# Two attention chunks in one row-tiled group, and PSUM banks named one by one, in a fused retention + MLP kernel

## The chip, the cores and the metric

The kernel runs on one core of a Trainium2 chip. The metric is the time of one execution on the device in microseconds (us). Smaller is better.

## The reference, cut to what matters

```python
# q, k, v: [B=8, H=8, S=576, D=64];  w_in: [512, 2048];  w_out: [2048, 512]
scores = (q @ k.T) / 8                            # per batch and head
ret    = scores * where(i >= j, gamma_h ** (i - j), 0)
x      = (ret @ v), heads side by side            # [4608 tokens, 512]
out    = gelu_exact(x @ w_in) @ w_out             # [4608, 512]
```

The kernel computes the retention part in chunks of 128 positions. A sequence of 576 has four full chunks and a short one of 64, so there are 40 chunks in all. Within a chunk it forms scores and multiplies them by v (the *inner* part). What came before the chunk enters through a running sum of k^T v (the *cross* part). The MLP goes through the 4608 tokens in nine blocks of 512, numbered 0 to 8.

## The kernel before

Three terms are needed. *PSUM* is where TensorE's results lie; the pools below share out its eight banks (2 + 2 + 1 + 3). *Row-tiled* means that a matmul uses 64 of the array's 128 rows, so that two of them, here of an even and an odd head, run side by side. The *mode* of the array is the rows*columns in use, as the profile prints it: 128*128 for the MLP and the inner parts, 64*128 for scores and cross parts, and 64*64 for those of short chunks.

TensorE's instructions come out in an order that a small scheduler in the kernel chooses while the program is built. It lays attention steps between MLP steps. Its kinds are T (turn q and k), R (scores), S (inner part and running sum), U (a cross part alone), V (scale v), X (turn x, for the first chunks) and the MLP steps "1" and "2". Cuts are marked with `...`.

```python
ps_sc  = tile_pool("ps_sc",  bufs=2, space=PSUM)   # two banks: scores of even and odd heads
ps_out = tile_pool("ps_out", bufs=1, space=PSUM)   # two banks: inner + cross of one chunk
ps_u   = tile_pool("ps_u",   bufs=1, space=PSUM)   # one bank: running sum
ps_mlp = tile_pool("ps_mlp", bufs=3, space=PSUM)   # three banks, oldest first: hT and oT

def scores(i):                                     # 64 rows of the array: row-tiled
    sc = [ps_sc.tile([128, HP, 128], FP32, tag="sc", ...) for e in range(2)]
    for hp in range(HP):
        for e in range(2):
            sl = slice(64 * e, 64 * e + 64)
            nc.tensor.matmul(sc[e][:cs, hp, :cs], lhsT=qkT[sl, 1, hp, :cs], rhs=qkT[sl, 0, hp, :cs], ...)

def cross(i):                                      # 64 rows as well
    for hp in range(HP):
        for e in range(2):
            sl = slice(64 * e, 64 * e + 64)
            nc.tensor.matmul(ov[:cs, e, hp, :], lhsT=s["qkT"][sl, 0, hp, :cs],
                             rhs=s["u"][sl, hp, 64 * e:64 * e + 64], start=False, ...)

def mlp1_step(t, m, lo, hi):                       # 16 tiles hT a block, 4 matmuls each
    hT = ps_mlp.tile([128, TOK_BLK], FP32, tag="mlp", name="hT")
    ...
    nc.scalar.activation(g_tiles[t, m][:, lo:hi], hT[:, :hi - lo], AF.Gelu)

def mlp2_step(t, ts, m0, m1):                      # 4 pieces of 128 tokens, 16 matmuls each
    if m0 == 0:
        acc[t, ts] = ps_mlp.tile([128, d_model], FP32, tag="mlp", name="oT")
    ...
    if m1 == N_DF:
        nc.scalar.copy(o_sb, oT)
        nc.sync.dma_start(out[row0:row0 + 128, :], o_sb)

# in the scheduler: one chunk's scores, then the cross part of the chunk before it
elif kind == "R":
    sc = scores(i)
    ...
    if open_ is not None:
        cross(open_)
    masked(i, sc)                                  # VectorE: scores to SBUF, masked
    ...
    if open_ is not None:
        close(open_)                               # VectorE: o_ps to SBUF, then transposed by DMA
```

## Time and profile before

| | |
|---|---|
| time | 315.15 us, median of 3 runs (314.97 to 315.23) |
| span of the profiled execution | 313.4 us |
| TensorE (PE) busy | 304.2 us, 97% |
| share of the chain that ended last on PE | 94% |

First come lines of the page of the kernel before: busy time and share of each engine, then the busy tenths of 40 slices, then the chain that ended last. PEld is TensorE's loading of weights, DVE is VectorE, ACT is ScalarE and POOL is GpSimd.

```profile
span 313.4 us, 6167 instructions
...
PE 304.2 (97%) x2522; PEld 166.3 (53%) x2522; DVE 102.9 (33%) x189; ACT 141.2 (45%) x279; POOL 112.3 (36%) x144
...
PE   7889998999999999999999999999999999999996
...
DMA  9999999999999999999989999698321221020012
...
PE 94%; DVE 3%; DMA 1%; issue 1%; ACT 0%; SPq 0%; DVEq 0%
```

A busy PE is not yet a PE at its peak, so the starts have to be read as well. Next is the timeline of the kernel before, PE alone, around the group of one full chunk. The columns are start (us from the span's start), duration (us), engine, line, operation, output and inputs, rows*columns of the array in use, shape and count. Here sc are scores, o_ps is a chunk's output, hT belongs to the first product of the MLP and oT to the second.

```profile
144.56 0.38 PE L323 MATMUL oT<-w_out_203,g_2374 128*128 128x512 bf16 x1
144.78 0.38 PE L323 MATMUL oT<-w_out_203,g_2381 128*128 128x512 bf16 x1
145.09 0.23 PE L211 MATMUL sc_2426<-qkT 64*128 64x128 bf16 x1
145.10 0.23 PE L211 MATMUL sc_2427<-qkT 64*128 64x128 bf16 x1
145.16 0.22 PE L211 MATMUL sc_2426<-qkT 64*128 64x128 bf16 x1
...
145.33 0.28 PE L262 MATMUL o_ps<-u_sb,qkT 64*128 64x64 bf16 x8
145.54 0.39 PE L323 MATMUL oT<-w_out_179,g_2211 128*128 128x512 bf16 x1
145.77 0.38 PE L323 MATMUL oT<-w_out_179,g_2218 128*128 128x512 bf16 x1
```

Read the starts, not the durations. Two 512-column matmuls start 216 ns apart (144.56 to 144.78). From the last of them to the first scores it is 312 ns, about 96 ns more. Scores start in twos, one for each half of the rows (145.09 and 145.10). At the group's end eight small matmuls take 213 ns, though a pair of them inside the group takes some 28 ns. That is the price of a change of the array's mode, paid on the way in and again on the way out. The Trainium skill, "TensorEngine Tiling (Array Packing)", Key Properties, says that changing the tiling mode drains TensorE; this trace fits that, with a loss of about 0.1 us at each change.

Last, the chain of waits of the kernel before at the passage from the first to the second product of block 7 (start, duration, engine, tile, line, count). PE follows PE with no other engine in between.

```profile
265.12 0.24 PE o_ps L262 x8
265.37 3.56 PE hT L296 x16
268.93 13.81 PE oT L323 x64
282.74 13.81 PE hT L296 x64
```

### The profile page before, as it was taken

The page shows a single profiled execution, that of the slowest core. Times are in us where ns is not written, and L with a number is a line of the kernel's source. Part 1 is how long each engine was busy: PE and PEld are TensorE (multiplying, and loading weights), DVE is VectorE, ACT ScalarE, POOL GpSimd, SP SyncE. Part 2 cuts the span into 40 slices and gives each one's busy share as a digit, 9 for nine tenths or more (in the row PEclk, how much of TensorE's full clock was granted, in tenths as well). Part 3 has the DMA queues.
Part 4 walks back from the last instruction along what each step waited for, and adds up shares of the span by engine and source line. Part 5 has one row for each costly group of instructions (what it writes and reads, how often), then busy time and mean ns, then how long its engine had stood idle before and what let it go on. Part 6 is the DMA issues. An engine that isn't in the chain of part 4 may idle for free.

```text
span 313.4 us, 6167 instructions
## 1 busy us (share of the span) xinstructions
PE 304.2 (97%) x2522; PEld 166.3 (53%) x2522; DVE 102.9 (33%) x189; ACT 141.2 (45%) x279; POOL 112.3 (36%) x144
## 2 busy tenths in 40 slices
PE   7889998999999999999999999999999999999996
PEld 3568655985645444444454444444454444444444
DVE  3740256737644334433142334423242322000000
ACT  5668303773427621662256224632564245316611
POOL 9956879384384074093309230440000000000000
PEclk9999999999999999999999999999999999999999
DMA  9999999999999999999989999698321221020012
GB/s 139 149 190 194 182 164 199 171 148 132 216 152 156 154 152 183 164 157 149 195 131 130 122 165 135 87 145 155 84 44 29 82 76 19 24 85 37 0 60 74
DMA packets 168636, 39.40 MB, mean 126 GB/s; under 512 B 157600, under 2 KB 164128, under 8 KB 168608
## 3 DMA queue, kind: packets, MB, share of 16 engines
q0 software_dynamic: 115792, 17.97, 87.4%
q1 hardware_dynamic: 52816, 21.05, 37.2%
q8 instruction: 19, 0.31, 0.4%
q14 instruction: 9, 0.07, 0.1%
HBM read 36.70 MB, written 9.44 MB: 147 GB/s over the span
## 4 chain that ended last, share of the span: by engine, by line
PE 94%; DVE 3%; DMA 1%; issue 1%; ACT 0%; SPq 0%; DVEq 0%
PE hT L296 40%; PE oT L323 39%; PE o_ps L242 3%; PE u_ps L248 2%; PE o_ps L262 2%; DMA k_101<-in_k_dram 1%; PE qk_ps L198 1%; PE oT L313 1%; DVE vh L227 1%; PE x_ps L284 0%; PE warm L434 0%; DVE ret_974 L220 0%; DVE ret_895 L220 0%; DVE ret_431 L220 0%; DVE ret_297 L220 0%
## 5 line engine op out<-in xcount | busy, mean ns | idle before, releaser
L135 POOL DMA_DIRECT2D qk_ld<-in_q_dram x39 | 33.8, 866 | 84.7 <-DMA qkT<-qk_ld 60.5
L327 ACT COPY o_sb<-oT 128x512 f32<-128x512 f32 x35 | 20.3, 587 | 93.6 <-PE oT L323 93.6
L135 POOL DMA_DIRECT2D v_ld<-in_v_dram x39 | 33.7, 864 | 6.2 <-DMA qk_ld<-in_k_dram 3.4
L270 DVE TENSOR_TENSOR x<-o_ps,dq 128x512 bf16<-128x512 f32 (+1 forms) x40 | 27.3, 681 | 21.7 <-PE o_ps L242 11.4
L135 POOL DMA_DIRECT2D qk_ld<-in_k_dram x39 | 33.5, 859 | 1.9 <-DMA v_ld<-in_v_dram 0.9
L252 ACT CAST u_sb<-u_ps 128x512 bf16<-128x512 f32 x32 | 18.8, 586 | 19.6 <-PE u_ps L248 19.6
L227 DVE TENSOR_TENSOR vh<-v_ld,dv 128x512 bf16<-128x512 bf16 x31 | 20.9, 679 | 0.0
L296 PE MATMUL hT<-xT,w_in_158 128*128 128x512 bf16 (+3 forms) x96 | 17.9, 326 | 0.0
L296 PE MATMUL hT<-xT,w_in_162 128*128 128x512 bf16 (+3 forms) x96 | 17.9, 326 | 0.0
L296 PE MATMUL hT<-xT,w_in_160 128*128 128x512 bf16 (+3 forms) x96 | 17.8, 326 | 0.0
L296 PE MATMUL hT<-xT,w_in_166 128*128 128x512 bf16 (+3 forms) x96 | 17.8, 326 | 0.0
L296 PE MATMUL hT<-xT,w_in_170 128*128 128x512 bf16 (+3 forms) x96 | 17.8, 326 | 0.0
L296 PE MATMUL hT<-xT,w_in_164 128*128 128x512 bf16 (+3 forms) x96 | 17.7, 326 | 0.0
L296 PE MATMUL hT<-xT,w_in_168 128*128 128x512 bf16 (+3 forms) x96 | 17.6, 326 | 0.0
L296 PE MATMUL hT<-xT,w_in_172 128*128 128x512 bf16 (+3 forms) x96 | 17.6, 326 | 0.0
L211 PEld LDWEIGHTS <-qkT 64*128 64x128 bf16 (+1 forms) x320 | 9.2, 98 | 12.5 <-issue 9.8
L296 PEld LDWEIGHTS <-w_in_172 128*128 128x128 bf16 x96 | 8.9, 98 | 7.1
L296 PEld LDWEIGHTS <-w_in_160 128*128 128x128 bf16 x96 | 8.9, 98 | 7.1
L248 PE MATMUL u_ps<-vh,qk_ld 128*128 128x128 bf16 x128 | 12.6, 222 | 0.0
L296 PEld LDWEIGHTS <-w_in_168 128*128 128x128 bf16 x96 | 8.8, 98 | 7.1
L296 PEld LDWEIGHTS <-w_in_164 128*128 128x128 bf16 x96 | 8.8, 98 | 6.9
L296 PEld LDWEIGHTS <-w_in_158 128*128 128x128 bf16 x96 | 8.5, 98 | 6.1
(814 smaller groups left out, 614.3 us busy)
## 6 DMA issues: line engine op xcount, KB each, us to landing
out_dram<-o_sb SPq DMA_DIRECT2D x35, 256.0 KB, 3.1
qk_ld<-in_q_dram POOLq DMA_DIRECT2D x31, 128.0 KB, 6.7
qk_ld<-in_k_dram POOLq DMA_DIRECT2D x31, 128.0 KB, 7.0
v_ld<-in_v_dram POOLq DMA_DIRECT2D x31, 128.0 KB, 7.1
qk_ld<-in_q_dram POOLq DMA_DIRECT2D x8, 64.0 KB, 6.7
qk_ld<-in_k_dram POOLq DMA_DIRECT2D x8, 64.0 KB, 6.5
v_ld<-in_v_dram POOLq DMA_DIRECT2D x8, 64.0 KB, 6.6
qkT<-qk_ld SPq DMA_TRANSPOSE x31, 7.7
```

Source lines behind the costliest of these rows:

```text
L135: nc.gpsimd.dma_start(dst[:cs], src[b, :, c0:c0 + cs, :].rearrange("h s d -> s h d"))
L198: nc.tensor.transpose(ps[:, hp, :cs], qk[:cs, j, 2 * hp:2 * hp + 2, :], ident[:cs, :cs])
L211: nc.tensor.matmul(sc[e][:cs, hp, :cs], lhsT=qkT[sl, 1, hp, :cs], rhs=qkT[sl, 0, hp, :cs], start=True, stop=True)
L227: nc.vector.tensor_tensor(vh[:cs], loaded[i][1][:cs], dv[:cs, :, ci:ci + 1].to_broadcast([cs, H, D]), op=ALU.mult)
L242: nc.tensor.matmul(ov[:, e, hp, :], lhsT=s["ret"][e][:, hp, :], rhs=s["vh"][:, 2 * hp + e, :], start=(hp == 0), stop=(ci == 0 and hp == HP ...
L248: nc.tensor.matmul(u_ps[0][:, hp, :], lhsT=loaded[i][0][:cs, 1, 2 * hp:2 * hp + 2, :], rhs=s["vh"][:cs, 2 * hp:2 * hp + 2, :], start=(ci = ...
L252: nc.scalar.copy(u, u_ps[0])
L262: nc.tensor.matmul(ov[:cs, e, hp, :], lhsT=s["qkT"][sl, 0, hp, :cs], rhs=s["u"][sl, hp, 64 * e:64 * e + 64], start=False, stop=(hp == HP - 1),
L270: nc.vector.tensor_tensor(x.rearrange("p hp e d -> p e hp d")[:cs], by_parity(s["o_ps"])[:cs], dq.rearrange("p (hp e) c -> p e hp c", e=2) ...
L296: nc.tensor.matmul(hT[:, :hi - lo], lhsT=w[:, cc, o:o + 128], rhs=xT[:, cc, tok0 + lo:tok0 + hi], start=(cc == 0), stop=(cc == N_DM - 1))
L323: nc.tensor.matmul(oT, lhsT=g_tiles[t, m][:, ts * 128:(ts + 1) * 128], rhs=w_out_sb[m // 2][:, m % 2, :], start=(m == 0), stop=(m == N_DF ...
L327: nc.scalar.copy(o_sb, oT)
```

## The change

The intent is to leave and enter the row-tiled mode less often. From chunk 18 on, within the second product, the scores of two chunks and the cross parts of the two chunks before them form one group. Ten pairs come about in this way. Two chunks' scores need four banks, so the pools are replaced by banks with names: a and b (scores), c, d, e (MLP), o (two banks) and u. While a pair stands in a, b, d and e, the second product's accumulator must lie on c. For the odd pieces it lies on a.

```diff
-    ps_sc / ps_out / ps_u / ps_mlp pools
+    ps = ctx.enter_context(tc.tile_pool(name="ps", bufs=1, space=PS))
+    def bank(of, shape, dtype, name):
+        while True:
+            tag = of[turns[of] % len(of)]
+            turns[of] += 1
+            if tag not in held:
+                break
+        last_tag[0] = tag
+        return ps.tile(shape, dtype, tag=tag, name=name)
@@ first product
-        hT = ps_mlp.tile([128, TOK_BLK], FP32, tag="mlp", name="hT")
+        hT = bank("cde", [128, TOK_BLK], FP32, "hT")
@@ second product
-            acc[t, ts] = ps_mlp.tile([128, d_model], FP32, tag="mlp", name="oT")
+            acc[t, ts] = bank("cde" if t < PAIR_FROM else "ca"[ts % 2], [128, d_model], FP32, "oT")
+            held.add(last_tag[0])
...
+            held.remove(acc_bank[t, ts])
@@ the scheduler
+            elif ts % 2 == 0 and 4 <= m0 <= 8 and ahead <= PAIR_LEAD:
+                if i + 1 < nxt["T"] and t < N_BLK - 1:
+                    got.append((max(r_at, at["R", i + 1]), "RR", i))
...
+            elif kind in ("R", "RR"):
+                mine = [i] if kind == "R" else [i, i + 1]
+                for j, bb in zip(mine, ("ab", "de")):
+                    sc.append(scores(j, bb))
...
+                for j in open_:
+                    if chunks[j][1] > 0:
+                        cross(j)
```

Cut: more buffers for the transposed q and k (9), scaled v (5), x (4) and the sum (4); an o_ps tile shared by a pair, one half each; v and transposes allowed further ahead from chunk 15 on; the scheduler's time estimates.

More of the change, by code (lines that the diff above doesn't have):

```diff
@@ L54 @@
     LEAD = 52
+    PAIR_FROM = 2
+    PAIR_LEAD = 70
+    LATE_LEAD = 48
     log_gamma = [math.log(1.0 - 2.0 ** (-5.0 - h)) for h in range(H)]
@@ L58 @@
     ld_pool = ctx.enter_context(tc.tile_pool(name="ld", bufs=N_LD))
-    tr_pool = ctx.enter_context(tc.tile_pool(name="tr", bufs=6))
+    tr_pool = ctx.enter_context(tc.tile_pool(name="tr", bufs=9))
     ret_pool = ctx.enter_context(tc.tile_pool(name="ret", bufs=2))
-    v_pool = ctx.enter_context(tc.tile_pool(name="v", bufs=3))
-    x_pool = ctx.enter_context(tc.tile_pool(name="x", bufs=3))
-    u_pool = ctx.enter_context(tc.tile_pool(name="u", bufs=2))
+    v_pool = ctx.enter_context(tc.tile_pool(name="v", bufs=5))
+    x_pool = ctx.enter_context(tc.tile_pool(name="x", bufs=4))
+    u_pool = ctx.enter_context(tc.tile_pool(name="u", bufs=4))
     g_pool = ctx.enter_context(tc.tile_pool(name="g", bufs=2))
@@ L67 @@
     PS = bass.MemoryType.PSUM
-    ps_sc = ctx.enter_context(tc.tile_pool(name="ps_sc", bufs=2, space=PS))
-    ps_out = ctx.enter_context(tc.tile_pool(name="ps_out", bufs=1, space=PS))
-    ps_u = ctx.enter_context(tc.tile_pool(name="ps_u", bufs=1, space=PS))
-    ps_mlp = ctx.enter_context(tc.tile_pool(name="ps_mlp", bufs=3, space=PS))
+    ps = ctx.enter_context(tc.tile_pool(name="ps", bufs=1, space=PS))
     xT = const_pool.tile([128, N_DM, n_tok], BF16, name="xT")
@@ L177 @@
     mlp_begun = [False]
+    turns = {"ab": 0, "cde": 0, "a": 0, "c": 0}
+    held = set()
+    last_tag = [None]
+    def bank(of, shape, dtype, name):
[6 more added lines that the diff above has]
+        return ps.tile(shape, dtype, tag=tag, name=name)
     def tr_ps(shape, name):
-        pool, tag = (ps_sc, "sc") if mlp_begun[0] else (ps_mlp, "mlp")
-        return pool.tile(shape, BF16, tag=tag, name=name)
+        return bank("ab" if mlp_begun[0] else "cde", shape, BF16, name)
     def turn(i, parts=(0, 1)):
@@ L202, in turn, with scores @@
                 nc.scalar.copy(qkT[:, j, :, :cs], ps[:, :, :cs])
-    def scores(i):
+    def scores(i, banks="ab"):
         cs = chunks[i][3]
         qkT = st[i]["qkT"]
-        sc = [ps_sc.tile([128, HP, 128], FP32, tag="sc", name=f"sc{e}") for e in range(2)]
+        sc = [ps.tile([128, HP, 128], FP32, tag=banks[e], name=f"sc{e}") for e in range(2)]
         for hp in range(HP):
@@ L229, in scaled_v, with by_parity, inner @@
         st[i]["vh"] = vh
-    def by_parity(o_ps):
-        return o_ps.rearrange("p e (hp d) -> p e hp d", d=D)[:, :, :HP]
-    def inner(i):
+    def by_parity(i):
+        lo = HP * st[i]["half"]
+        return st[i]["o_ps"].rearrange("p e (hp d) -> p e hp d", d=D)[:, :, lo:lo + HP]
+    def inner(i, mate=None):
         b, ci, c0, cs = chunks[i]
         s = st[i]
-        s["o_ps"] = ps_out.tile([128, 2, 512], FP32, tag="o_ps", name="o_ps")
-        ov = by_parity(s["o_ps"])
+        s["half"] = 0 if mate is None else 1
+        s["o_ps"] = ps.tile([128, 2, 512], FP32, tag="o", name="o_ps") if mate is None else st[mate]["o_ps"]
+        ov = by_parity(i)
         for e in range(2):
@@ L242, in inner @@
                 nc.tensor.matmul(ov[:, e, hp, :], lhsT=s["ret"][e][:, hp, :], rhs=s["vh"][:, 2 * hp + e, :],
-                                 start=(hp == 0), stop=(ci == 0 and hp == HP - 1), skip_group_check=True)
+                                 start=(hp == 0 and mate is None), stop=(ci == 0 and hp == HP - 1), skip_group_check=True)
         if ci + 1 < NCH:
             if ci == 0:
-                u_ps[0] = ps_u.tile([128, HP, 128], FP32, tag="u_ps", name="u_ps")
+                u_ps[0] = ps.tile([128, HP, 128], FP32, tag="u", name="u_ps")
             for hp in range(HP):
@@ L257, in cross @@
         s = st[i]
-        ov = by_parity(s["o_ps"])
+        ov = by_parity(i)
         for hp in range(HP):
@@ L270, in evacuate @@
         nc.vector.tensor_tensor(
-            x.rearrange("p hp e d -> p e hp d")[:cs], by_parity(s["o_ps"])[:cs],
+            x.rearrange("p hp e d -> p e hp d")[:cs], by_parity(i)[:cs],
             dq.rearrange("p (hp e) c -> p e hp c", e=2)[:cs, :, :, ci:ci + 1].to_broadcast([cs, 2, HP, D]),
@@ L300, in mlp1_step @@
         nc.scalar.activation(g_tiles[t, m][:, lo:hi], hT[:, :hi - lo], AF.Gelu)
-    acc = {}
+    acc, acc_bank = {}, {}
     def mlp2_step(t, ts, m0, m1):
@@ L310, in mlp2_step @@
             for lo, hi in ((0, 256), (256, 384), (384, 512)):
-                oT = ps_mlp.tile([128, d_model], FP32, tag="mlp", name="oT")
+                oT = bank("cde", [128, d_model], FP32, "oT")
                 for m in range(N_DF):
@@ L319, in mlp2_step @@
         if m0 == 0:
-            acc[t, ts] = ps_mlp.tile([128, d_model], FP32, tag="mlp", name="oT")
+            acc[t, ts] = bank("cde" if t < PAIR_FROM else "ca"[ts % 2], [128, d_model], FP32, "oT")
+            held.add(last_tag[0])
+            acc_bank[t, ts] = last_tag[0]
         oT = acc[t, ts]
@@ L335 @@
     half = [0]
-    open_ = None
+    open_ = []
+    group = {}
     to_turn = []
@@ L400, in attention_picks @@
         i = nxt["S"]
-        if i < min(nxt["R"], nxt["V"]) and open_ is None:
+        if i < min(nxt["R"], nxt["V"]) and (not open_ or open_[0] in group[i]):
             got.append((at["S", i], "S", i))
@@ L406, in attention_picks @@
             r_at = at["R", i]
-            if paced >= 32 * tok(i) / TOK_BLK - LEAD:
-                got.append((r_at, "R", i))
-        if open_ is not None and (nxt["R"] == N_CH or open_ < N_FIRST or (open_ < N_PE_TR and r_at > now + 1.2)):
-            got.append((at["U", open_], "U", open_))
+            ahead = 32 * tok(i) / TOK_BLK - paced
+            pick = mlp_pick()
+            kind, t, ts, m0, _ = pick[1][0] if pick is not None else ("2", N_BLK, 0, 0, 0)
+            if pick is None or t < PAIR_FROM:
+                if ahead <= LEAD:
+                    got.append((r_at, "R", i))
+            elif kind == "1" or (t == N_BLK - 1 and ts == 3):
+                if ahead <= LATE_LEAD:
+                    got.append((r_at, "R", i))
+            elif ts % 2 == 0 and 4 <= m0 <= 8 and ahead <= PAIR_LEAD:
+                if i + 1 < nxt["T"] and t < N_BLK - 1:
+                    got.append((max(r_at, at["R", i + 1]), "RR", i))
+                elif ahead <= LATE_LEAD or i == N_CH - 1:
+                    got.append((r_at, "R", i))
+        if open_ and nxt["S"] == nxt["R"]:
+            if nxt["R"] == N_CH or open_[0] < N_FIRST or (open_[0] < N_PE_TR and r_at > now + 1.2):
+                got.append((at["U", open_[-1]], "U", open_[-1]))
         i = nxt["V"]
-        if i < nxt["T"] and i < nxt["S"] + 2:
+        if i < nxt["T"] and i < nxt["S"] + (2 if i < 15 else 4):
             got.append((land_chunk[i][2] + 0.2, "V", i))
         i = nxt["T"]
-        if i < N_CH and i in land_chunk and i <= nxt["S"] + (2 if i < N_PE_TR else 4):
+        if i < N_CH and i in land_chunk and i <= nxt["S"] + (2 if i < N_PE_TR else 4 if i < 15 else 5):
             if i >= N_FIRST:
@@ L431, in warm @@
     def warm(n):
-        w = ps_mlp.tile([128, 512], FP32, tag="mlp", name="warm")
+        w = bank("cde", [128, 512], FP32, "warm")
         for _ in range(n):
@@ L449 @@
             elif kind == "S":
-                inner(i)
+                mates = group[i]
+                inner(i, mates[0] if i != mates[0] else None)
                 nxt["S"] += 1
@@ L454 @@
                     load_chunk(i + N_LD, now)
-                if chunks[i][1] > 0:
-                    open_ = i
+                if chunks[i][1] > 0 or len(mates) > 1:
+                    open_.append(i)
                     at["U", i] = now
@@ L459 @@
                     close(i)
-            elif kind == "R":
-                sc = scores(i)
-                nxt["R"] += 1
-                now += 0.19 + 0.22 * f
-                if open_ is not None:
-                    cross(open_)
-                    now += 0.12
-                masked(i, sc)
-                at["S", i] = now + (1.9 if i < N_FIRST else 3.2 if i < N_PE_TR else 2.3 if i < 16 else 2.8)
-                if open_ is not None:
-                    close(open_)
-                    open_ = None
-            elif kind == "U":
-                cross(i)
-                now += 0.31
-                close(i)
-                open_ = None
+            elif kind in ("R", "RR"):
+                mine = [i] if kind == "R" else [i, i + 1]
+                sc = []
+                for j, bb in zip(mine, ("ab", "de")):
+                    group[j] = mine
+                    sc.append(scores(j, bb))
+                    now += 0.22 * chunks[j][3] / C
+                now += 0.2
+                nxt["R"] += len(mine)
+                for j in open_:
+                    if chunks[j][1] > 0:
+                        cross(j)
+                        now += 0.13
+                masked(mine[0], sc[0])
+                at["S", i] = now + (1.9 if i < N_FIRST else 3.2 if i < N_PE_TR else 2.3 if i < 16 else 2.8)
+                for j in open_:
+                    close(j)
+                open_ = []
+                if len(mine) > 1:
+                    at["S", i] = now + 3.4
+                    at["S", i + 1] = now + 4.7
+                    masked(mine[1], sc[1])
+            elif kind == "U":
+                now += 0.2
+                for j in open_:
+                    if chunks[j][1] > 0:
+                        cross(j)
+                        now += 0.12
+                for j in open_:
+                    close(j)
+                open_ = []
             elif kind == "V":
@@ L520 @@
         now = min(waits)
-    assert nxt["S"] == N_CH and open_ is None and not to_turn
+    assert nxt["S"] == N_CH and not open_ and not to_turn
 _INS = ['q', 'k', 'v', 'moe_w_in', 'moe_w_out']
```

## The prediction

> **What bounds the kernel now.** TensorE. The chain of waits puts 94% of the 313.4 us span on it, and from 94 us on the timeline shows its matmuls back to back: 128x512 matmuls start every 216 ns, with no wait for another engine. DMA is 90% busy up to 220 us (slices), but nothing on TensorE waits for it after 94 us. So only TensorE's own time counts.
>
> **What a row-tiled group costs.** Scores and cross parts use 64 rows of the array. The Trainium skill, "TensorEngine Tiling (Array Packing)", Key Properties, says that a change of tiling mode drains TensorE. The trace agrees: before a full scores group the last 512-column matmul takes 312 ns to the next start, not 216 (+96). Eight scores take 234 ns, eight cross parts and the way back 213 ns, of which some 112 is work (28 ns a pair), so about +100. Changes to and from the short chunks' 64x64 mode cost 93 to 130.
>
> **What the change removes.** Matmul counts stay the same. By the order of instructions, ten pairs are formed (18/19, 20/21, 22/23, 24/25, 27/28, 29/30, 31/32, 33/34, 36/37, 38/39); 26 and 35 stay single. The program's mode changes fall from 104 to 88. Priced with the costs above (19, 20, 6, 5, 4, 5 changes of each kind before; 13, 10, 2, 5, 8, 5 after) this is about 1.56 us less, all on the critical path.
>
> **What it adds.** Accumulators of the second product are now pinned to bank c (even 128-row pieces) or a (odd), instead of taking the oldest bank. The first product still rotates c, d, e, sixteen tiles per block, so the last tile before the second product falls on c in two blocks (t=4 and t=7). There the first matmul must wait for that tile's Gelu. In the trace a last hT matmul's start is followed by Gelu's start 0.415 us later, 0.60 us of Gelu, and some 0.04 us to TensorE: 1.06 us, against 0.22 in t=7 (a stall of about 0.84) and 0.67 in t=4, where an inner group stands between (about 0.39). In block 1, holding banks lets a first-product tile take a bank whose output copy is pending: I count stalls of 0.29 and 0.83 us where before had 0.06 and 0.60: +0.46. Sum: about +1.7 us. VectorE's longer chain (four masks, two evacuations, 0.60 us apart, 4 us) fits into the 3.5 us of matmuls before the first inner part plus 0.9 us of group; x transposes still have over 10 us. The scores of 18/19 need two transposed chunks at once; before they landed at 106.7 and 108.9 us, for use near 110: tight but enough.
>
> **Prediction.** -1.56 + 1.7, plus 0.05 of near misses: 315.3 us, range 314.2 to 316.7. Faster by over 2%: 0.01; within 2%: 0.97; slower: 0.02.
>
> **What would show it.** Right: pairs of score groups with one +96 ns entry; TensorE idle of about 0.8 us before the second product of block 7 and 0.4 us in block 4, released by ScalarE's Gelu; idle before two narrow hT groups in block 1, released by the output copy; no idle before scores. Wrong on savings: paired groups longer than about 0.9 us for full chunks.
>
> **What would make it wrong.** Upwards: the transposes of 19 or 21 landing late (earlier transposes compete with loads), so that scores wait on DMA; a paired group starving TensorE's queue of small matmuls; the running sum's copy late for the second inner part. Downwards: bank stalls cheaper than counted, leaving up to 1.5 us of gain.

## The result, and the profile after

| | runs | median, us | range, us |
|---|---|---|---|
| before | 4 | 315.06 | 314.50 to 315.23 |
| changed | 4 | 315.10 | 314.44 to 315.61 |

The ratio is 1.0003, with a 95% interval of 0.9978 to 1.0028: the same time. Before's fourth run joins the three above.

The same lines of the changed kernel's page:

```profile
span 312.7 us, 6134 instructions
...
PE 301.3 (96%) x2522; PEld 165.3 (53%) x2522; DVE 102.1 (33%) x189; ACT 142.3 (45%) x279; POOL 112.4 (36%) x144
...
PE   7799997999999999999999999999999999999996
...
DMA  9999999999999999999999999929403140021012
...
PE 90%; DMA 3%; POOL 2%; DVE 2%; ACT 1%; issue 1%; DVEq 0%
```

PE is busy 2.9 us less, yet the span is only 0.7 us shorter, and ACT appears in the chain with 1%. Idle time has taken the place of work. Only 1.4 of the 2.9 us lie in the stretch that is compared below (243.1 us busy before, 241.8 after, of 243.9); the rest, and the 3% of DMA and 2% of POOL in the chain, lie in the first 60 us, which differ from run to run.

The timeline of the changed kernel, PE alone, around a paired group:

```profile
140.77 0.38 PE L344 MATMUL oT<-w_out_172,g_2259 128*128 128x512 bf16 x1
141.08 0.23 PE L226 MATMUL sc_2354<-qkT 64*128 64x128 bf16 x1
...
141.31 0.22 PE L226 MATMUL sc_2364<-qkT 64*128 64x128 bf16 x1
...
141.48 0.22 PE L226 MATMUL sc_2365<-qkT 64*128 64x128 bf16 x1
141.53 0.28 PE L280 MATMUL o_ps<-u_sb,qkT 64*128 64x64 bf16 x8
141.75 0.39 PE L344 MATMUL oT<-w_out_174,g_2266 128*128 128x512 bf16 x1
```

The way in costs 0.31 us once (140.77 to 141.08). The second chunk's scores (sc_2364, 141.31) follow the first's with no gap at all. Counted in the order of the matmuls in the traces, changes of mode are 104 before and 88 now.

The chain of waits of the changed kernel at the passage to the second product, in block 4 and then in block 7:

```profile
171.91 0.61 ACT g_2745 L318
172.56 1.02 PE oT L344 x4
...
253.70 13.83 PE hT L314 x64
267.55 0.61 ACT g_3892 L318
268.19 13.97 PE oT L344 x64
```

A Gelu on ACT (g_2745, g_3892) now stands between the two products, where before PE followed PE. From start to start, the step into block 7's second product takes 1064 ns, not 216.

The waits of PE on ACT for banks of the MLP, changed kernel (what waited, for what, us in total, times, longest):

```profile
PE hT L314 <- ACT o_sb L349: 0.9, 2, 0.7
PE oT L344 <- ACT g_3892 L318: 0.7, 1, 0.7
...
PE oT L344 <- ACT g_2745 L318: 0.2, 1, 0.2
```

The kernel before has one such line in its waits:

```profile
PE oT L323 <- ACT o_sb L327: 0.4, 1, 0.4
```

These waits count from the modelled end of the matmul before, so they come out smaller than the time lost. The time lost is the difference of starts: 0.85, 0.39, 0.84 and 0.29 us in the changed kernel, 0.60 and 0.06 us before.

### A stretch that can be compared to a hundredth of a microsecond

The first 60 us depend on when loads land. In the ten profiled executions, chunk 8's inner part starts at 61.8 to 63.4 us. That spread is larger than most of the effects to be explained. From there on PE waits for no DMA in any of the ten, so the stretch from there to the first of the narrow last pieces is used below. It is split at chunk 15's inner part, read from the starts of PE's matmuls, one profiled execution per kernel. Kernels that are alike in a part agree there to 0.01 us: 31.42 or 31.43 in four of them, 211.28 in e1_order and e5_clean. All differences in the number of mode changes lie inside the stretch. The traces of the last four runs lack 36 or 37 of the 2522 matmul records, but none of the starts used here.

| kernel | chunk 8 to 15, us | chunk 15 to the last pieces, us | sum, us | against before |
|---|---|---|---|---|
| before | 30.96 | 212.99 | 243.95 | |
| changed | 31.43 | 212.51 | 243.94 | -0.01 |
| e1_order | 31.43 | 211.28 | 242.71 | -1.24 |
| e2_split | 31.42 | 214.12 | 245.54 | +1.59 |
| e3_pinned | 31.42 | 215.27 | 246.69 | +2.74 |
| e4_all_c | 32.26 | 215.83 | 248.09 | +4.14 |
| e5_clean | 30.96 | 211.28 | 242.24 | -1.71 |
| e6_full_mode | 31.05 | 210.96 | 242.01 | -1.94 |
| e7_full_mode_single | 30.58 | 211.86 | 242.44 | -1.51 |
| e8_best | 30.58 | 209.73 | 240.31 | -3.64 |

Gain and loss cancel: before and after differ by 0.01 us over 244 us.

### The profile page after: what moved, and what is told of

It is laid out like the page before. It is cut to its first block, busy times and chain, and to the rows that moved or that the text cites. A ratio compares the mean times of both kernels' runs of the same rounds, so it can differ in the third digit from the quotient of the medians. Undisturbed runs are those within 1.5% of the kernel's fastest.

```text
span 312.7 us, 6134 instructions
## 1 busy us (share of the span) xinstructions
PE 301.3 (96%) x2522; PEld 165.3 (53%) x2522; DVE 102.1 (33%) x189; ACT 142.3 (45%) x279; POOL 112.4 (36%) x144
## 4 chain that ended last, share of the span: by engine, by line
PE 90%; DMA 3%; POOL 2%; DVE 2%; ACT 1%; issue 1%; DVEq 0%
PE hT L314 40%; PE oT L344 38%; PE o_ps L260 3%; PE u_ps L266 2%; DMA v_ld<-in_v_dram 2%; PE o_ps L280 2%; DMA qk_ld<-in_q_dram 1%; PE oT L331 1%; POOL qk_ld L136 1%; PE qk_ps L213 1%; DVE vh L242 0%; ACT o_sb L349 0%; PE x_ps L302 0%; POOL v_ld L136 0%; DVE ret_422 L235 0%
## 5 line engine op out<-in xcount | busy, mean ns | idle before, releaser
L288 DVE TENSOR_TENSOR x<-o_ps,dq 128x512 bf16<-128x512 f32 (+1 forms) x40 | 26.4, 681 | 16.6 <-PE o_ps L280 10.4
```

What stands on the lines that cost most here:

```text
L288: nc.vector.tensor_tensor(x.rearrange("p hp e d -> p e hp d")[:cs], by_parity(i)[:cs], dq.rearrange("p (hp e) c -> p e hp c", e=2)[:cs, :, ...
```

## The experiments

The theory: the pairs save about 0.1 us for each mode change that falls away, and PE's new waits on ScalarE for banks c (later blocks) and c, d, e (block 1) give it all back. The rival: the pairs save next to nothing, and the new waits only stand where time would have been lost anyway. Each experiment ran in five rounds beside the kernel before. The outputs are right. The first four shared one chip and 11 runs of before (median 315.28 us), the last four another 11 (median 314.93 us).

### e1_order: take the later waits away

```diff
         mlp_begun[0] = True
+        if m == 0 and t >= PAIR_FROM:
+            turns["cde"] = 2
         hT = bank("cde", [128, TOK_BLK], FP32, "hT")
@@ the narrow last pieces
+            turns["cde"] = 1
             for lo, hi in ((0, 256), (256, 384), (384, 512)):
```

> The changed kernel with one thing altered: at the start of each block from block 2 on, the first product's bank rotation is set so that its last two tiles lie on d and e, never on c (and the narrow last pieces start on d). Pairs, order of matmuls and number of mode changes stay. Theory (pairs save about 1.5 us, waits for Gelu on bank c give 1.2 us of it back): the idle times of 0.39 and 0.85 us before the second product of blocks 4 and 7 vanish, 1.23 us less than the changed kernel, near 313.9 us, ratio to before about 0.996. Rival (the pairs save next to nothing; the waits only take the place of slack that would appear elsewhere): unchanged, 315.1 us, ratio 1.000.

Measured: 314.16 us (313.59 to 315.51), ratio 0.9958 (0.9932 to 0.9984). The stretch is 1.23 us shorter than the changed kernel's, as the theory said. In the waits of PE no Gelu of a first product is left, and the two waits of block 1 remain:

```profile
PE hT L316 <- ACT o_sb L352: 0.9, 2, 0.7
```

So the two waits of blocks 4 and 7 were real costs, caused by the choice of the bank and by nothing else: order and amount of work are untouched. The rival's second half falls.

### e2_split: make two groups of every pair again

```diff
                 for j, bb in zip(mine, ("ab", "de")):
                     group[j] = mine
+                    if j != i:
+                        _, t, a, b_, c_ = mlp_pick()[1].pop(0)
+                        mlp2_step(t, a, b_, c_)
+                        now += MM * (c_ - b_)
+                        paced += (c_ - b_) / 4
                     sc.append(scores(j, bb))
```

> The changed kernel with four 512-column matmuls of the second product put between the scores of the two chunks of every pair, so that each pair is two row-tiled groups again; bank naming and its waits stay. Theory: each pair pays one more way in and out of the row-tiled mode, so mode changes rise from 88 to 103 and the time by about 1.5 us, to near 316.6 us, ratio to before about 1.005, with the 0.39 and 0.85 us waits still there. Rival (pairing saves nothing): 315.1 us, ratio 1.000.

Measured: 317.33 us (316.39 to 318.20), ratio 1.0060 (1.0034 to 1.0085). The stretch is 1.60 us longer than the changed kernel's, for 15 more mode changes (103 in the trace): 0.107 us each. The timeline of PE shows the second way in:

```profile
141.64 1.03 PE L344 MATMUL oT<-w_out,g 128*128 128x512 bf16 x4
142.60 0.40 PE L226 MATMUL sc<-qkT 64*128 64x128 bf16 x8
142.93 1.04 PE L344 MATMUL oT<-w_out,g 128*128 128x512 bf16 x4
143.90 0.40 PE L226 MATMUL sc<-qkT 64*128 64x128 bf16 x8
```

Four matmuls at 216 ns are 0.86 us, but from the first to the second line it is 0.96 us and from the third to the fourth 0.97 us. Pairing does save what it was meant to; the rival's first half falls.

### e3_pinned: the bank rule alone, without pairs

The kernel before with named banks that skip held ones, and accumulators pinned from block 2 on. They lie on c and d in turn, since single groups use a and b everywhere. The diff is cut to the accumulators; the rotation is that of the change.

```diff
-            acc[t, ts] = ps_mlp.tile([128, d_model], FP32, tag="mlp", name="oT")
+            if t < 2:
+                acc[t, ts] = bank([128, d_model], FP32, "oT")
+            else:
+                last_tag[0] = "cd"[ts % 2]
+                acc[t, ts] = ps_mlp.tile([128, d_model], FP32, tag=last_tag[0], name="oT")
+            held.add(last_tag[0])
+            acc_bank[t, ts] = last_tag[0]
```

> The kernel before (single groups, 104 mode changes) with only the bank rule of the change carried over: accumulators hold a named bank, rotation skips held ones, and from block 2 on the accumulators are pinned, here to c and d in turn, because single groups need a and b for scores. Theory: no pairs, no saving; the bank waits alone cost about +0.36 us in block 1 (0.29 and 0.83 in place of 0.06 and 0.60) and about 0.3, 0.3, 0.84 and 0.84 us in later blocks, +2.6 us in all: near 317.7 us, ratio 1.008. Rival (bank waits are hidden): 315.1 us, ratio 1.000.

Measured: 317.38 us (316.88 to 318.06), ratio 1.0064 (1.0039 to 1.0089); the stretch is 2.74 us longer than before's. The part from chunk 8 to 15, in which block 1's waits lie, takes 31.42 us where before takes 30.96, as in the changed kernel (31.43). So the bank rule alone brings that loss, and the pairs have no part in it.

### e4_all_c: the suspected wait in every block

```diff
+        if m == 0 and t >= PAIR_FROM:
+            turns["cde"] = 0
         hT = bank("cde", [128, TOK_BLK], FP32, "hT")
```

> The changed kernel with the rotation set so that the last tile of the first product falls on c in every block from 2 to 8, the accumulator's bank: the suspected wait, multiplied. Theory: waits of 0.39 us where an inner part stands in between (three blocks) and 0.84 us where none does (four blocks), and 0.84 us at the start of block 2 on the output copy: about 4.1 us more than the changed kernel, near 319.2 us, ratio to before about 1.013. Rival (those waits are hidden or cheap): 315 to 316 us.

Measured: 319.73 us (318.61 to 321.30), ratio 1.0136 (1.0105 to 1.0166). The stretch is 4.15 us longer than the changed kernel's, against 4.1 expected. The waits of PE now count seven Gelus and three output copies:

```profile
PE oT L346 <- ACT g L320: 3.4, 7, 0.7
PE hT L316 <- ACT o_sb L351: 1.6, 3, 0.7
```

### e5_clean: pairs without any new wait

e1_order, with block 2 starting its rotation on d and with the bank that an accumulator has just left taken last in block 1.

```diff
         if m == 0 and t >= PAIR_FROM:
-            turns["cde"] = 2
+            turns["cde"] = 1 if t == 2 else 2
@@ second product
             held.remove(acc_bank[t, ts])
+            if t == 1 and ts < 3:
+                turns["cde"] = "cde".index(acc_bank[t, ts]) + 1
```

> The changed kernel with pairs and pinned accumulators kept and all new bank waits taken away by choosing the rotation: last tiles of the first product off bank c, and in block 1 a bank that an accumulator has just left is taken last. Theory: what remains is the pairs' saving alone, 16 mode changes at about 0.107 us: the stretch from chunk 15's inner part to the last narrow tiles is 211.3 us as in the run with the order altered, the stretch before it (chunk 8's to chunk 15's inner part) is back at 30.96 us; near 313.5 us, ratio to before about 0.9945. Rival (some other cost of the pairs was hidden behind the waits and now comes out): no better than the run with the order altered, 314.2 us.

Measured: 313.23 us (313.11 to 314.09), ratio 0.9950 (0.9927 to 0.9972). Both parts of the stretch came out as written down: 30.96 and 211.28 us. The pairs alone are worth 1.71 us, which is 0.107 us for each of 16 mode changes. No hidden cost of the pairs came out. In the waits of PE, what is left on ScalarE is the one that the kernel before has as well:

```profile
PE oT L347 <- issue: 1.1, 7, 0.2
PE oT L347 <- ACT o_sb L354: 0.4, 1, 0.4
```

The seven waits for "issue" are no new waits: each stands where the record of a matmul is missing after a group (349 ns from start to start, the 123 and 226 ns of two steps).

### e6_full_mode and e7_full_mode_single: fewer mode changes by another way

Short chunks used 64 of 128 columns of the array, which is a mode of its own. This experiment gives them all 128 columns. Their second half computes values that nobody reads.

```diff
+    qkT_short = [const_pool.tile([128, 2, HP, 128], BF16, name=f"qkT_short{n}") for n in range(2)]
@@ turn
-            st[i]["qkT"] = tr_pool.tile([128, 2, HP, 128], BF16, tag="qkT", name="qkT")
+            if cs < C:
+                st[i]["qkT"] = qkT_short[b % 2]
+                if b < 2:
+                    nc.vector.memset(qkT_short[b], 0.0)
+            else:
+                st[i]["qkT"] = tr_pool.tile([128, 2, HP, 128], BF16, tag="qkT", name="qkT")
@@ scores
-                nc.tensor.matmul(sc[e][:cs, hp, :cs], lhsT=qkT[sl, 1, hp, :cs], ...
+                nc.tensor.matmul(sc[e][:, hp, :cs], lhsT=qkT[sl, 1, hp, :], ...
@@ cross
-                nc.tensor.matmul(ov[:cs, e, hp, :], lhsT=s["qkT"][sl, 0, hp, :cs], ...
+                nc.tensor.matmul(ov[:, e, hp, :], lhsT=s["qkT"][sl, 0, hp, :], ...
```

On the changed kernel (bank waits left in):

> The changed kernel with one thing altered: short chunks use all 128 columns for scores and cross parts (their transposed q and k lie in two tiles of their own, zeroed once), so the 64x64 mode never occurs and a group has one way in and one way out. Bank waits stay. Theory (each change of mode costs about 0.1 us on TensorE, whatever the modes): mode changes fall from 88 to 72, about 1.7 to 2.1 us less than the changed kernel, near 313.2 us, ratio to before about 0.994. Rival (only the way between full array and row tiling costs; changes within a group are free): 315.1 us, ratio 1.000.

Measured: 312.70 us (312.45 to 313.56), ratio 0.9933 (0.9910 to 0.9957). The stretch is 1.93 us shorter than the changed kernel's, for 16 fewer changes (72 in the trace): 0.12 us each.

On the kernel before, with single groups and the old pools:

> The kernel before, single groups, with only the short chunks' full-column mode: mode changes fall from 104 to 92. Theory: about 1.3 to 1.6 us less than before, near 313.7 us, ratio 0.9955, with no pairs and no bank rule at all. Rival (the pairs, not the number of changes, bring the time): 315.2 us, ratio 1.000.

Measured: 313.47 us (312.46 to 314.39), ratio 0.9952 (0.9925 to 0.9978). The stretch is 1.51 us shorter than before's, for 12 fewer changes (92 in the trace), 0.126 us each. The timelines of PE around a short chunk's group, in the kernel before and then in this one:

```profile
152.70 0.38 PE L323 MATMUL oT<-w_out_203,g_2381 128*128 128x512 bf16 x1
153.01 0.21 PE L211 MATMUL sc_2515<-qkT 64*64 64x64 bf16 x1
...
153.13 0.19 PE L211 MATMUL sc_2516<-qkT 64*64 64x64 bf16 x1
153.25 0.29 PE L262 MATMUL o_ps<-u_sb,qkT 64*128 64x64 bf16 x8
153.47 0.39 PE L323 MATMUL oT<-w_out_179,g_2211 128*128 128x512 bf16 x1
```

```profile
151.06 0.38 PE L330 MATMUL oT<-w_out,g 128*128 128x512 bf16 x1
151.37 0.29 PE L218 MATMUL sc<-qkT_short 64*128 64x64 bf16 x8
151.49 0.28 PE L269 MATMUL o_ps<-u_sb,qkT 64*128 64x64 bf16 x8
151.71 1.25 PE L330 MATMUL oT<-w_out,g 128*128 128x512 bf16 x4
```

From the scores' start to the cross part's it was 0.24 us (153.01 to 153.25) and is 0.12 us now (151.37 to 151.49), with twice as many columns in use. A change between 64*64 and 64*128 inside a group costs about what a way in costs: 125 ns from the last 64*64 start to the next, where pairs otherwise follow every 29 ns, so some 96. The number of changes is not all, though. In 64*64 the first pair takes 53 ns to the next and the others 32; in 64*128 it is 39 and 29, some 20 ns less for a group of four pairs. For the 14 such groups of the stretch that is an estimated 0.28 us, which leaves some 0.10 us for each change in both experiments. Neither pairs nor banks are needed for this gain.

### e8_best: all three

> Pairs, bank order without new waits, and short chunks in the full-column mode, together. Theory (the parts add up): mode changes 72, no new waits: about 1.7 us less than before by the pairs, 1.7 to 2.1 us by the mode: near 311.5 us, ratio to before about 0.988. Rival (another limit, the transposes or loads, comes up once TensorE is faster): above 312.5 us, with TensorE idle before scores or first-product tiles that a DMA ends.

Measured: 311.64 us (310.89 to 312.18), ratio 0.9892 (0.9866 to 0.9918): faster than before by 1.1%, with an interval clear of 1, though short of the 2% that counts as faster here. The stretch is 3.64 us shorter, which is the sum of e5_clean's 1.71 and the 1.93 of the full mode. The parts add up, and no wait of PE on a DMA appears in the stretch; the rival, another limit, did not come up.

Over all eight experiments, the medians of the runs came within 0.8 us of the times expected, and the stretches within 0.15 us of the differences expected.

## Why the prediction was right

The prediction was 315.3 us, range 314.2 to 316.7; measured were 315.1 us.

- **What bounds the kernel.** Right. In all eight experiments what was added to PE's path or taken from it showed up in full in the stretch.
- **The saving of the pairs.** Right in mechanism, a little small in size. 1.56 us were predicted, 1.71 measured (e5_clean). The mis-sized term was the price of a mode change, taken as 0.098 us on average where it is 0.107. The starts show what was left out: after a change the first step is longer too. The first 512-column matmul after a group takes some 226 ns to the next start, not 216 (145.54 to 145.77 in the lines of before), and the first pair of a full chunk's scores 67 ns, not 56. With the 96 ns of the change that makes some 106 ns, and 10 ns for each of 16 changes is 0.16 us, about the 0.15 us that were missed.
- **The waits in blocks 4 and 7.** Right: 0.39 and 0.85 us measured, 0.39 and 0.84 predicted, released by the Gelu that was named. e1_order and e4_all_c show that the bank choice alone makes them.
- **The waits in block 1.** Right: 0.29 and 0.84 us, against 0.29 and 0.83 predicted, +0.47 us on the stretch against +0.46. e3_pinned has the same loss without any pair.
- **Near misses, 0.05 us.** None was seen in the starts. Tiles with a gap of about 1.08 us (five starts of 216 ns) between the last matmul on a bank and the next owner did not wait, which fits a need of 1.06 us.
- **VectorE's longer chain, the transposes of chunks 18 and 19.** Right: no PE idle time before any paired scores, and the late transposes that were named as a risk did not come about. One thing was not foreseen. VectorE stood 5.9 us waiting for v of a later chunk, just before the mask of chunk 17, because v is now scaled further ahead. It cost nothing, since the inner part that needs the mask came 3.9 us after the scores.

The predicted time was a difference of two terms, -1.56 and +1.7. The measured terms are -1.71 and +1.71 (0.47, 0.39 and 0.85), so the small total is no accident of errors cancelling: each term was measured by itself. That 315.3 and 315.1 us lie so close is partly luck, for the interval of the measured ratio alone is some 0.8 us to either side.

What stays open: the first 60 us vary by about 1.6 us between executions, in every kernel. That was not studied. It hides differences below some 0.3% from the run times, which is why the stretch was needed.

## What to carry to other kernels

When TensorE is the limit and a change of the array's mode costs 0.1 us, count the changes in the order of instructions. Grouping small matmuls is one way to cut them, and letting short tiles use the full number of columns is a simpler one; the two gains add up. When a rotating buffer is replaced by pinned or held ones, check who owned that bank last at every hand-over. The oldest bank has had the longest time to come free (before lost 0.66 us on it, in block 1), while a pinned one may have been written 0.2 us ago, and here pinning and holding together gave back the whole gain. A result of "no change" can be two real effects of equal size, so look for idle time that has a new releaser.

## What the Trainium skill lacked or had wrong

- "TensorEngine Tiling (Array Packing)", Key Properties, says that a change of tiling mode drains TensorE and gives no price. Here it is 0.107 us a change on average when groups were joined or split (e2_split, e5_clean). Removing the 64x64 mode of short chunks gave 1.93 us for 16 changes and 1.51 us for 12, of which an estimated 0.28 us is the slower pairs of that mode, so some 0.10 us a change.
- The same page's Performance Considerations advise column tiling for a stationary free dimension of 64 or less. They do not say what it costs where no second column tile is packed beside the first, as with the short chunks here: without that mode the kernel before became 0.48% faster (e7_full_mode_single).
- "PSUM — Partial Sum Buffer", Summary, says to evacuate promptly. It has no figure for how soon a bank can be written again. From the start of the last 512-column matmul on a bank, through ScalarE's Gelu or copy, to TensorE's next start on it were 1.05 to 1.10 us here (1064 ns with a Gelu in block 7, 1052 ns with a copy in block 1).
